# Turning an expert unit's outputs with one VectorE instruction and five transfers through DRAM

## The chip, the cores and the metric

The kernel runs on one core of a Trainium2 chip. The metric is device time in microseconds (us), lower is better. The engines named below are TensorE (PE; its weight loads are listed apart as PEld), VectorE (DVE), ScalarE (ACT), GpSimd (POOL) and SyncE (SP), which issues most of the transfers.

## The reference

Block-sparse attention (4 batches, 8 heads, 768 positions, head size 64, float32) is followed by a mixture of 8 experts without dropped tokens. The second part matters here:

```
x        = attention output as (3072, 512)
logits   = x @ w_gate                       # (3072, 8)
expert   = argmax(logits);  gate = softmax(logits)[expert]
for e in 8 experts:                         # rows grouped by expert
    y[rows of e] = relu(x[rows of e] @ w1[e]) @ w2[e]    # 512 -> 1024 -> 512
out = gate * y                              # in the rows' own order
```

Everything is float32. How many rows an expert gets is known only when the kernel runs.

## The kernel before

The attention part runs to about 358 us and writes its rows, with the gate as a 513th column, to a DRAM tensor `x_rows`. Then the rows are worked off in *units*, each a set of at most 512 rows of one expert: two `early` units of 256 rows, then `whole` units of 384 rows (here three, called unit0 to unit2), then one `own` unit per expert (own0 to own7) with what is left of that expert. The own units stand in a `tc.Switch` on their width, so that PE and ACT run code for the width that is needed; here it is 176, 128, 256, 128, 256, 160, 352 and 160 rows.

A unit goes through these steps, each a method of `Unit`:

- `gather` (L672): POOL fetches up to 4 x 128 rows from `x_rows` by index into the tile `xg`, rows on partitions.
- `fetch` (L686): SP fetches `w1` and `w2` of the expert, 2 MB each. Two pairs of buffers alternate.
- `turn` (L689, L697): DVE keeps the gates and turns the rows with 16 transposes of 32x32 blocks, into `xT` with features on partitions.
- `layer1` (L712, L716): 32 matmuls with `w1` as weights, relu on ACT into `hT`. The trace counts 64 for them, since it lists each float32 matmul twice.
- `layer2` (L725, L729): as many matmuls with 128 adjacent columns of `w2` as weights, output features on partitions, copied by ACT into `zT`.
- `finish` (L748, L753, L734): DVE turns `zT` back with 16 transposes into `zo`, POOL multiplies each group of 128 rows by the gates and puts it into the output by index. `zo` is one buffer.

The last unit, own7, uses `layer2_by_rows` (L765, L768, L734), whose outputs already have rows on partitions, so it has no `finish`.

PE, DVE and POOL are scheduled by hand: each executes its instructions in the order in which the code is written. SP is not; the scheduler orders it. The own loop's body is, for unit e: gather of e+2, the Switch with the two layers, `turn` of e+2, both fetches of e+2, `finish` of e. The buffers `xg`, `xT`, `zT` alternate from unit to unit. One `xg`, one `xT` and both `zT` are pieces of a large tile shown as `ar`; `hT` and `zo` are pieces of one shown as `ea`. So L697 has the two forms `xT<-ar` and `ar<-xg`.

Of the kernel before, what the change touches and what calls it, by code (L numbers as in the profile page):

```python
# [17 lines left out]
def kernel(  # L18
# [11 lines left out]
    nc = tc.nc  # L30
# [38 lines left out]

    x_d = nc.dram_tensor("x_rows", (N, XW), F32, kind="Internal").ap()  # L70


# [118 lines left out]
    by_hand = ExitStack()  # L191
    by_hand.enter_context(tc.manual_schedule(engines={mybir.EngineType.Pool, mybir.EngineType.PE, mybir.EngineType.DVE}))
    make_mask(make_mask_pool.enter_context(tc.tile_pool(name="mk", bufs=1)))
# [48 lines left out]
    def attend(n, half, c):  # L242
        v_sb = loaded[pairs[n]][2]
        if c == 0:

            ops_[(n, half)] = rt["bank"] = ps_o.tile([P, 512], F32, name="op")
        op = ops_[(n, half)][:, :CW]
        e = es[(n, half, c)]
        for hh in range(2):
            nc.tensor.matmul(  # L250
                op[hh * D : (hh + 1) * D, :], lhsT=v_sb[:, hh, c, :], rhs=e[:, hh, :], start=(c == 0), stop=(c == NCH - 1),
            )
        if c == NCH - 1:
            oT = work.tile([P, CW], F32, name="oT", bufs=4)
            nc.scalar.copy(oT[:], op)  # L255
            ops_[(n, half)] = oT

    def divide(n, half):

        oT, esum = ops_[(n, half)], esums.pop((n, half))  # L260
        sp = ps_x.tile([P, CW], F32, name="sp", tag="xr")
        for hh in range(2):
            nc.tensor.matmul(sp[hh * D : (hh + 1) * D, :], lhsT=ones[:], rhs=esum[:, hh, :], start=True, stop=True)
        ss = work.tile([P, CW], F32, name="ss")
        nc.scalar.activation(ss[:], sp[:], AF.Copy, bias=1e-9)  # L265
        row = 2 * (2 * n + half)
        nc.sync.dma_start(sums[row : row + 2, :], ss.rearrange("(h d) q -> h d q", h=2)[:, 0, :])
        r = work.tile([P, CW], F32, name="r")
        for m in range(HC):
            nc.vector.reciprocal(r[:, m * P : (m + 1) * P], ss[:, m * P : (m + 1) * P])  # L270
        nc.vector.tensor_mul(oT[:], oT[:], r[:])
# [381 lines left out]
    w2s = [wp.tile([P, FB, DM], F32, name=f"w2_{j}") for j in range(2)]  # L653
    xgs = [wp.tile([P, RJ, XW], F32, name="xg0")[:]]
    xTs = [wp.tile([P, DB, RW], F32, name="xT0")[:]]
# [3 lines left out]
    zo = flat[:, FB * RW : FB * RW + RJ * DM].rearrange("p (j d) -> p j d", j=RJ)  # L659
    zTs = [ar[:, j * DB * RW : (j + 1) * DB * RW].rearrange("p (c t) -> p c t", c=DB) for j in range(2)]  # L660
    xTs.append(ar[:, 2 * DB * RW : 3 * DB * RW].rearrange("p (c t) -> p c t", c=DB))
    xgs.append(ar[:, 3 * DB * RW : 3 * DB * RW + RJ * XW].rearrange("p (j w) -> p j w", j=RJ))

    class Unit:

        def __init__(self, ph, col, nj, at, expert, xg, xT, w, zT):
            self.ph, self.col, self.nj, self.at, self.expert = ph, col, nj, at, expert
            self.xg, self.xT, self.w1, self.w2, self.zT = xg, xTs[xT], w1s[w], w2s[w], zTs[zT]

        def gather(self):  # L670
# [49 lines left out]
        def layer2(self, n, between={}):  # L720

            for d in range(DB):
                zp = upper["banks"][(FB + d) % 6]
                for fb in range(FB):
                    nc.tensor.matmul(  # L725
                        zp[:, :n], lhsT=self.w2[:, fb, d * P : (d + 1) * P], rhs=hT[:, fb, :n],
                        start=(fb == 0), stop=(fb == FB - 1),
                    )
                nc.scalar.copy(self.zT[:, d, :n], zp[:, :n])  # L729
                for do in between.get(d, []):  # L730
                    do()
# [10 lines left out]

        def finish(self, group):

            for tq in range(4):
                for dq in range(4):
                    t, d = slice(tq * 32, (tq + 1) * 32), slice(dq * 32, (dq + 1) * 32)
                    nc.vector.transpose(  # L748
                        zo[t, : self.nj, :].rearrange("p j (c q d) -> p j c q d", c=DB, q=4)[:, :, :, dq, :],
                        self.zT[d].rearrange("p c (j q t) -> p j c q t", j=RJ, q=4)[:, : self.nj, :, tq, :],  # L750
                    )
            for j in range(self.nj):
                nc.gpsimd.tensor_scalar(  # L753
                    zo[:, j, :], zo[:, j, :], scalar1=gates[:, self.at, j : j + 1], scalar2=None, op0=ALU.mult,
                )
                self.put(j, zo[:, j, :], group)
# [32 lines left out]
    for i, (n, half) in enumerate(steps):  # L789
# [35 lines left out]
        if n + 1 == len(pairs) and half == 1:  # L825
# [3 lines left out]
            for j in range(QA // P):  # L829
                early[0].turn_by_matmul(j, tp[:, j])  # L830
    divide(*steps[-1])
    banks(lent)
# [11 lines left out]
    def tokens_b():  # L844
        judge()
        tokens("B", NT, NB_)
        whole(0, 0).fetch(1)
        whole(0, 0).gather()
        own[0].gather()

    rows_out(n, 0)
    early[0].layer1(QA, {2: [lambda: rows_out(n, 1)], 5: [turn_1], 7: [count_b]})
    early[0].layer2(QA)
    early[1].layer1(QA, {1: [tokens_b]})
    whole(0, 0).fetch(2)
    own[0].fetch(1)
    early[1].layer2(QA)
    own[0].fetch(2)
    whole(0, 0).turn()
    own[0].turn()  # L860
    for u in early:
        u.finish("rows_out")
    by_hand.close()

    lent.close()
    for arm in tc.Switch(nc.values_load(rt["arm"][0:1, 0:1], min_val=0, max_val=REDO), REDO + 1):
        inside = ExitStack()
        if arm <= UM:
            inside.enter_context(tc.manual_schedule(engines={mybir.EngineType.Pool, mybir.EngineType.PE, mybir.EngineType.DVE}))
            pools = inside.enter_context(ExitStack())  # L870
            banks(pools)
            units = [whole(i, arm - 1) for i in range(arm)]
            for u, then in zip(units, units[1:] + [own[1]]):
# [5 lines left out]
                then.fetch(2)  # L879
                u.finish("rows_out")  # L880
            if not units:
                own[1].gather()
                own[1].turn()
                own[1].fetch(1)
                own[1].fetch(2)
        else:
# [7 lines left out]
            for part in range(2):  # L894
                one_hots("A", rt["slA"], TA, EA * QA // P, part)
            tokens("A", TA, EA * QA // P)
            ranks("B", TA, NT)
# [3 lines left out]
            for u, width in [(u, QA) for u in early] + [(whole(i, i), UW) for i in range(UM)] + [(u, RW) for u in own]:  # L901
# [5 lines left out]
                u.layer2(width)  # L907
                u.finish("rows_again")

# [3 lines left out]
    banks(lent)  # L913
    by_hand.enter_context(tc.manual_schedule(engines={mybir.EngineType.Pool, mybir.EngineType.PE, mybir.EngineType.DVE}))
    ET = mybir.EngineType
    for e, u in enumerate(own):
        if e + 2 < E:
            own[e + 2].gather()
        at = rt["size"][0:1, e : e + 1]
# [6 lines left out]
        for k in tc.Switch(index, (RW - P) // GR + 1):  # L926
# [4 lines left out]
            else:  # L931
                u.layer2_by_rows(width, "rows_out")
        if e + 2 < E:
            own[e + 2].turn()
            own[e + 2].fetch(1)
            own[e + 2].fetch(2)
        if e + 1 < E:
            u.finish("rows_out")
    by_hand.close()
# [31 lines left out]
```

## Time and profile before

| | us |
|---|---|
| median of 3 runs | 899.52 |
| range of the runs | 899.34 to 901.68 |
| profiled execution, device time | 897.08 |
| profiled execution, span | 895.4 |
| PE busy in the span | 742.2 (83%) |
| DVE busy | 535.9 (60%) |
| POOL busy | 164.2 (18%) |

The span runs from the first to the last recorded instruction or transfer; all trace times are counted from its start. [...] A row's idle time names what ended it; "issue" there means that the engine waited for nothing that the profile shows.

### The profile page before, as it was taken

The numbers are of one execution on the slowest core, as the hardware profiler recorded it, in microseconds if no ns is written. First come the engines' busy times: TensorE is split into PE (matmuls) and PEld (weight loads), VectorE is DVE, ScalarE is ACT, GpSimd is POOL, SyncE is SP. The second block draws the span as 40 slices with busy tenths as digits, with TensorE's granted clock in tenths as the row PEclk, the third lists the DMA queues.
The fourth block names the chain that finished last, engine by engine and source line by source line (L and its number), as shares of the span: only waits on it lengthen the run. The fifth ranks groups of instructions, "written<-read, shape, count | busy, mean of one in ns | idle before, by whom it ended". The sixth has DMA issues, their size and how long they took to land. (4 is left out here: it accounts for less than half of the span.)

```text
span 895.4 us, 11949 instructions
## 1 busy us (share of the span) xinstructions
PE 742.2 (83%) x4516; PEld 481.7 (54%) x4516; DVE 535.9 (60%) x858; ACT 288.8 (32%) x516; POOL 164.2 (18%) x175
## 2 busy tenths in 40 slices
PE   7999999999999999999977999865970757189820
PEld 4555555555555555878544555864870657056600
DVE  4777787777777998478626443536272736363650
ACT  3666666666666665211101110110110101011100
POOL 4000000000000002011233131312314242323333
PEclk8999999999999999999998999976986797579875
DMA  7233232223222382155351434555454072402000
GB/s 160 71 80 80 74 73 72 72 72 73 72 72 72 112 320 78 26 207 167 134 183 67 142 117 155 195 182 197 147 180 157 12 250 84 159 14 59 18 13 35
DMA packets 98451, 99.74 MB, mean 111 GB/s; under 512 B 57491, under 2 KB 73939, under 8 KB 98324
## 3 DMA queue, kind: packets, MB, share of 16 engines
q1 hardware_dynamic: 89152, 79.50, 28.3%
q0 software_dynamic: 7040, 18.29, 6.5%
q8 instruction: 61, 1.00, 0.5%
q10 hardware_dynamic: 2132, 0.41, 0.2%
q14 instruction: 66, 0.54, 0.2%
HBM read 85.40 MB, written 17.66 MB: 115 GB/s over the span
## 5 line engine op out<-in xcount | busy, mean ns | idle before, releaser
L725 PE MATMUL bank<-ea,w 128*128 128x256 f32 (+5 forms) x768 | 170.8, 383 | 0.0
L229 PE MATMUL s<-ar 64*128 64x384 f32 x768 | 158.7, 492 | 0.9 <-ACT ar L214 0.9
L712 PE MATMUL bank<-xT,w 128*128 128x384 f32 (+3 forms) x512 | 121.6, 405 | 40.4 <-DVE xT L697 31.5
L234 ACT ACTIVATE ea<-s 128x768 f32<-128x768 f32 x192 | 152.4, 812 | 6.3 <-PE s L232 3.4
L725 PEld LDWEIGHTS bank<-ea,w 128*128 128x128 f32 x768 | 130.3, 191 | 38.8
L748 DVE STREAM_TRANSPOSE ea<-ar 32x512 f32<-32x512 f32 (+2 forms) x192 | 120.0, 625 | 35.9 <-DMA out_dram<-ea,sB 13.0
L712 PE MATMUL bank<-ar,w 128*128 128x256 f32 (+2 forms) x320 | 82.2, 423 | 64.9 <-DVE ar L697 51.4
L240 DVE TENSOR_TENSOR esum<-esum,ea 128x768 f32<-128x768 f32 x128 | 122.7, 958 | 14.1 <-ACT ea L234 0.5
L250 PE MATMUL op<-ea,ar 128*64 128x384 f32 x768 | 129.3, 486 | 0.0
L712 PEld LDWEIGHTS bank<-xT,w 128*128 128x128 f32 x512 | 91.2, 217 | 70.3 <-DVE xT L697 30.0
L716 ACT ACTIVATE ea<-bank 128x256 f32<-128x256 f32 (+5 forms) x104 | 38.8, 381 | 272.5 <-PE bank L712 249.9
L753 POOL TENSOR_SCALAR ea<-ea,gates 128x512 f32<-128x512 f32 x41 | 64.5, 1573 | 301.6 <-DVE ea L748 248.4
L712 PEld LDWEIGHTS bank<-ar,w 128*128 128x128 f32 x320 | 65.3, 214 | 80.7 <-DVE ar L697 51.8
L250 PEld LDWEIGHTS op<-ea,ar 128*64 128x64 f32 x768 | 55.1, 137 | 68.8 <-issue 68.8
L229 PEld LDWEIGHTS s<-ar 64*128 64x128 f32 x768 | 67.0, 190 | 38.1 <-issue 34.2
L270 DVE RECIPROCAL r<-ss 128x128 f32<-128x128 f32 x96 | 82.2, 911 | 2.5 <-ACT ss L265 2.5
L689 DVE COPY gates<-ar 128x4 f32<-128x4 f32 (+1 forms) x7 | 1.2, 170 | 125.3 <-DMA ar<-x_rows,gB 125.3
L697 DVE STREAM_TRANSPOSE xT<-ar 32x512 f32<-32x512 f32 (+1 forms) x112 | 72.3, 645 | 2.2
L240 DVE TENSOR_TENSOR esum<-ea 128x768 f32<-128x768 f32 x32 | 30.6, 957 | 63.4 <-ACT ea L234 63.4
L729 ACT COPY ar<-bank 128x256 f32<-128x256 f32 (+5 forms) x48 | 18.0, 375 | 149.9 <-PE bank L725 147.7
L232 PE MATMUL s<-pen,oh 64*128 64x384 bf16 x384 | 63.1, 325 | 0.0
L255 ACT COPY oT<-op 128x384 f32<-128x384 f32 x32 | 15.3, 478 | 106.3 <-PE op L250 106.3
(200 smaller groups left out, 455.4 us busy)
## 6 DMA issues: line engine op xcount, KB each, us to landing
w<-in_moe_w_dram SPq DMA_DIRECT2D x26, 2048.0 KB
ar<-in_k_dram SPq DMA_DIRECT2D x32, 192.0 KB
ar<-in_v_dram SPq DMA_DIRECT2D x16, 384.0 KB
x_rows<-xb SPq DMA_DIRECT2D x16, 384.0 KB
ar<-in_q_dram SPq DMA_DIRECT2D x30, 192.0 KB
out_dram<-ea,sB POOLq DMA_INDIRECT x37
sums<-ss SPq DMA_DIRECT2D x32, 3.0 KB
ar<-x_rows,gB POOLq DMA_INDIRECT x25
```

The costliest lines, as they stand in the source:

```text
L229: nc.tensor.matmul(s[:, hh, :CW], lhsT=kT[r, c * P : (c + 1) * P], rhs=qT[r, cols], start=True, stop=False)
L232: nc.tensor.matmul(s[:, hh, :CW], lhsT=oh[r, c, :], rhs=pen[r, cols], start=False, stop=True)
L234: nc.scalar.activation(e, s[:, :, :CW], AF.Exp, scale=scale)
L240: nc.vector.tensor_add(t[:], es[(n, half, 0)] if c == 1 else t[:], e)
L250: nc.tensor.matmul(op[hh * D : (hh + 1) * D, :], lhsT=v_sb[:, hh, c, :], rhs=e[:, hh, :], start=(c == 0), stop=(c == NCH - 1),)
L270: nc.vector.reciprocal(r[:, m * P : (m + 1) * P], ss[:, m * P : (m + 1) * P])
L697: nc.vector.transpose(self.xT[d].rearrange("p c (j q t) -> p j c q t", j=RJ, q=4)[:, : self.nj, :, tq, :], self.xg[t, : self.nj, :DM].rear ...
L712: nc.tensor.matmul(hp[:, :n], lhsT=self.w1[:, c, fb * P : (fb + 1) * P], rhs=self.xT[:, c, :n], start=(c == 0), stop=(c == DB - 1),)
L716: nc.scalar.activation(hT[:, fb, :n], hp[:, :n], AF.Relu)
L725: nc.tensor.matmul(zp[:, :n], lhsT=self.w2[:, fb, d * P : (d + 1) * P], rhs=hT[:, fb, :n], start=(fb == 0), stop=(fb == FB - 1),)
L748: nc.vector.transpose(zo[t, : self.nj, :].rearrange("p j (c q d) -> p j c q d", c=DB, q=4)[:, :, :, dq, :], self.zT[d].rearrange("p c (j q ...
L753: nc.gpsimd.tensor_scalar(zo[:, j, :], zo[:, j, :], scalar1=gates[:, self.at, j : j + 1], scalar2=None, op0=ALU.mult,)
```

## The change

`finish` is split. `turn_back` turns all of `zT` with a single DVE instruction into `zq`, in which each 32x32 block is transposed but stays in its group of 32 partitions. Its four column groups then go by four transfers, one from each group of 32 partitions, to their places in a DRAM tensor `z_rows`, and a fifth transfer loads `z_rows` into `zo`, rows on partitions. `leave` multiplies by the gates, now on DVE, and puts the rows. For the columns to come out in order, `layer2` takes every fourth column of `w2` as one set of 128 weights, so a weight load reads its floats 16 bytes apart, and `turn_back` writes with the same step.

There are two separate `xg` buffers. In the own loop the gather is issued for unit e+3 and stands ahead of the puts of unit e; the order on DVE becomes `turn_back` of e, `turn` of e+2, `leave` of e. SP is ordered by hand as well: the fetches of e+2 stand before the five transfers of e. Ahead of the units, `oT` has 3 buffers for 4, `r` 1 for 2, and the tokens of the second phase are worked out after block 3 and no longer after block 1 of the second early unit's first layer.

```diff
+    z_d = nc.dram_tensor("z_rows", (2, RW, DM), F32, kind="Internal").ap()
...
-            oT = work.tile([P, CW], F32, name="oT", bufs=4)
+            oT = work.tile([P, CW], F32, name="oT", bufs=3)
...
-        r = work.tile([P, CW], F32, name="r")
+        r = work.tile([P, CW], F32, name="r", bufs=1)
...
-    xgs = [wp.tile([P, RJ, XW], F32, name="xg0")[:]]
+    xgs = [wp.tile([P, RJ, XW], F32, name=f"xg{j}")[:] for j in range(2)]
...
+    zq = parts[3].rearrange("p (g d) -> p g d", g=4 * RJ)
...
-                        zp[:, :n], lhsT=self.w2[:, fb, d * P : (d + 1) * P], rhs=hT[:, fb, :n],
+                        zp[:, :n], lhsT=self.w2[:, fb, :].rearrange("p (d c) -> p c d", c=DB)[:, d, :], rhs=hT[:, fb, :n],
...
-        def finish(self, group):
-
-            for tq in range(4):
-                for dq in range(4):
-                    t, d = slice(tq * 32, (tq + 1) * 32), slice(dq * 32, (dq + 1) * 32)
-                    nc.vector.transpose(
-                        zo[t, : self.nj, :].rearrange("p j (c q d) -> p j c q d", c=DB, q=4)[:, :, :, dq, :],
-                        self.zT[d].rearrange("p c (j q t) -> p j c q t", j=RJ, q=4)[:, : self.nj, :, tq, :],
-                    )
+        def turn_back(self):
+
+            g = 4 * self.nj
+            nc.vector.transpose(
+                zq[:, :g, :].rearrange("p g (d c) -> p c g d", c=DB),
+                self.zT[:, :, : 32 * g].rearrange("p c (g t) -> p c g t", t=32),
+            )
+            for a in range(4):
+                nc.sync.dma_start(
+                    self.z_d[: 32 * g, a * P : (a + 1) * P].rearrange("(g t) d -> t g d", t=32), zq[a * 32 : (a + 1) * 32, :g, :],
+                )
+            nc.sync.dma_start(zo[:, : self.nj, :], self.z_d[: 32 * g].rearrange("(j p) d -> p j d", p=P))
+
+        def leave(self, group):
             for j in range(self.nj):
-                nc.gpsimd.tensor_scalar(
+                nc.vector.tensor_scalar(
                     zo[:, j, :], zo[:, j, :], scalar1=gates[:, self.at, j : j + 1], scalar2=None, op0=ALU.mult,
                 )
                 self.put(j, zo[:, j, :], group)
...
+    by_hand.enter_context(tc.manual_schedule(engines={mybir.EngineType.SP}))
     divide(*steps[-1])
...
-    early[1].layer1(QA, {1: [tokens_b]})
-    whole(0, 0).fetch(2)
+    first.fetch(2)
+    early[0].turn_back()
+    early[1].layer1(QA, {3: [tokens_b]})
     own[0].fetch(1)
     early[1].layer2(QA)
     own[0].fetch(2)
-    whole(0, 0).turn()
+    first.turn()
+    early[0].leave("rows_out")
+    early[1].turn_back()
     own[0].turn()
-    for u in early:
-        u.finish("rows_out")
+    early[1].leave("rows_out")
...
-                u.finish("rows_out")
+                u.turn_back()
+                if then is own[1]:
+                    own[2].gather()
+                u.leave("rows_out")
...
     for e, u in enumerate(own):
-        if e + 2 < E:
-            own[e + 2].gather()
...
+        if e + 3 < E:
+            own[e + 3].gather()
         if e + 2 < E:
-            own[e + 2].turn()
             own[e + 2].fetch(1)
             own[e + 2].fetch(2)
         if e + 1 < E:
-            u.finish("rows_out")
+            u.turn_back()
+        if e + 2 < E:
+            own[e + 2].turn()
+        if e + 1 < E:
+            u.leave("rows_out")
```

On DVE, two rounds of the own loop before the change; a branch marks the end of a round, L689 and L697 are `turn`, L748 is `finish`:

```order
L689 COPY gates<-ar 128x4
L697 STREAM_TRANSPOSE xT_178<-ar 32x4x4x32 x16
L748 STREAM_TRANSPOSE ea<-ar 32x16x32 x16
L966 UNCONDITIONAL_BRANCH
L689 COPY gates<-xg_177 128x4
L697 STREAM_TRANSPOSE ar<-xg_177 32x4x4x32 x16
L748 STREAM_TRANSPOSE ea<-ar 32x16x32 x16
L966 UNCONDITIONAL_BRANCH
```

and two rounds after it, where L751 is `turn_back`, L694 and L702 are `turn`, and L763 is the multiplication in `leave`, which the list shows in the stretch that follows its branch:

```order
L763 TENSOR_SCALAR ea<-ea,gates 128x512 x4
L751 STREAM_TRANSPOSE ar<-ar 128x4x512
L694 COPY gates<-xg_178 128x4
L702 STREAM_TRANSPOSE xT_179<-xg_178 32x4x4x32 x16
L988 UNCONDITIONAL_BRANCH
L763 TENSOR_SCALAR ea<-ea,gates 128x512 x4
L751 STREAM_TRANSPOSE ar<-ar 128x4x512
L694 COPY gates<-xg_177 128x4
L702 STREAM_TRANSPOSE ar<-xg_177 32x4x4x32 x16
L988 UNCONDITIONAL_BRANCH
```

The turning back of a unit stood behind the turn of the unit two ahead and stands before it now; its 16 instructions are one, and four multiplications have come from POOL.

On POOL, one round of the own loop before, with the multiplications (L753), puts (L734) and gather (L672):

```order
L753 TENSOR_SCALAR ea<-ea,gates 128x512
L734 DMA out_dram<-ea,sB 3072x512
L753 TENSOR_SCALAR ea<-ea,gates 128x512
L734 DMA out_dram<-ea,sB 3072x512
L753 TENSOR_SCALAR ea<-ea,gates 128x512
L734 DMA out_dram<-ea,sB 3072x512
L753 TENSOR_SCALAR ea<-ea,gates 128x512
L734 DMA out_dram<-ea,sB 3072x512
L672 DMA ar<-x_rows,gB 128x520 x4
L966 UNCONDITIONAL_BRANCH
```

and two rounds after, puts (L739) and gathers (L677):

```order
L739 DMA out_dram<-ea,sB 3072x512 x4
L677 DMA xg_177<-x_rows,gB 128x520 x4
L988 UNCONDITIONAL_BRANCH
L739 DMA out_dram<-ea,sB 3072x512 x4
L677 DMA xg_178<-x_rows,gB 128x520 x4
L988 UNCONDITIONAL_BRANCH
```

POOL's rounds hold no arithmetic any more, and what follows the puts of a unit is the gather for the unit four further on, where it was the one for three further on.

## Rows read from the trace of the kernel before

**Rows 1.** Timeline of PE, 455 to 870 us: start, length, line, operation, count, idle before.

```profile
474.72 22.83 PE L712 MATMUL bank<-xT,w 128*128 128x384 f32 x64 [9.49 <-DVE xT L697]
...
518.03 20.80 PE L712 MATMUL bank<-xT,w 128*128 128x384 f32 x64
...
573.95 9.84 PE L725 MATMUL bank<-ea,w 128*128 128x176 f32 x64
591.91 10.34 PE L712 MATMUL bank<-xT,w 128*128 128x128 f32 x64 [8.11 <-issue]
602.08 7.31 PE L725 MATMUL bank<-ea,w 128*128 128x128 f32 x64
619.86 16.79 PE L712 MATMUL bank<-ar,w 128*128 128x256 f32 x64 [10.47 <-DVE ea L748]
...
655.81 9.18 PE L712 MATMUL bank<-xT,w 128*128 128x128 f32 x64 [5.35 <-DVE xT L697]
...
699.32 16.34 PE L712 MATMUL bank<-ar,w 128*128 128x256 f32 x64 [27.18 <-DVE ar L697]
...
743.21 11.43 PE L712 MATMUL bank<-xT,w 128*128 128x160 f32 x64 [13.75 <-DVE xT L697]
754.48 8.86 PE L725 MATMUL bank<-ea,w 128*128 128x160 f32 x64
787.53 21.72 PE L712 MATMUL bank<-ar,w 128*128 128x352 f32 x64 [24.19 <-DVE ar L697]
...
831.11 11.84 PE L712 MATMUL bank<-xT,w 128*128 128x160 f32 x64 [2.92 <-DVE xT L697]
```

**Rows 2.** Who waited for whom, 560 to 860 us: us in total, times, longest.

```profile
POOL ea L753 <- DVE ea L748: 168.0, 6, 30.2
...
DVE gates L689 <- DMA xg<-x_rows,gB: 66.2, 3, 24.9
...
PE bank L712 <- DVE ar L697: 51.4, 2, 27.2
```

**Rows 3.** Timeline of DVE, 680 to 896 us, columns as in rows 1.

```profile
687.75 0.17 DVE L689 COPY gates<-xg 128x4 f32<-128x4 f32 x1 [20.25 <-DMA xg<-x_rows,gB]
687.83 11.44 DVE L697 STREAM_TRANSPOSE ar<-xg 32x512 f32<-32x512 f32 x16
699.29 11.71 DVE L748 STREAM_TRANSPOSE ea<-ar 32x512 f32<-32x512 f32 x16
...
855.77 11.71 DVE L748 STREAM_TRANSPOSE ea<-ar 32x512 f32<-32x512 f32 x16 [13.02 <-DMA out_dram<-ea,sB]
```

**Rows 4.** Timeline of POOL, 560 to 896 us.

```profile
683.42 0.95 POOL L672 DMA_INDIRECT xg<-x_rows,gB  x1 [0.31 <-issue]
...
867.58 1.56 POOL L753 TENSOR_SCALAR ea<-ea,gates 128x512 f32<-128x512 f32 x1 [13.06 <-DVE ea L748]
869.42 1.02 POOL L734 DMA_INDIRECT out_dram<-ea,sB  x1 [0.28 <-POOL ea L753]
...
883.51 0.98 POOL L734 DMA_INDIRECT out_dram<-ar,sB  x1 [0.30 <-issue]
```

**Rows 5.** Timeline of ACT, its last instruction.

```profile
856.84 0.68 ACT L768 ACTIVATE ar<-bank,gates 32x512 f32<-32x512 f32 x1 [6.30 <-PE bank L765]
```

**Rows 6.** DVE by line and shape, 240 to 400 us: busy us, mean ns, idle.

```profile
L511 DVE TENSOR_REDUCE slA<-slot 128x18 f32<-128x144 f32 x1 | 0.4, 399 | 0.0
...
L378 DVE TENSOR_SCALAR ok<-sums 64x384 f32<-64x384 f32 x1 | 0.3, 345 | 0.0
...
L441 DVE TENSOR_REDUCE best<-sc 128x18 f32<-128x144 f32 x1 | 0.3, 303 | 0.0
```

**Rows 7.** Weight loads by line and shape, 380 to 860 us.

```profile
L633 PEld LDWEIGHTS <-orB 128*128 128x128 bf16 x24 | 1.3, 103 | 1.3 <-issue 1.3
```

**Rows 8.** Busy time by stage: each engine, then clock, DMA share, GB/s.

```profile
560.00:592.00 32.00, 20.84 (x128) 20.33 (x126) 11.29 (x20) 3.22 (x12) 11.71 (x10) 0.88 0.66 232
...
743.00:788.00 45.00, 20.59 (x129) 20.35 (x130) 23.20 (x35) 3.59 (x12) 14.31 (x12) 0.69 0.34 121
```

More of the change, by code (lines that the diff above doesn't have):

```diff
@@ L191 @@
     by_hand = ExitStack()
-    by_hand.enter_context(tc.manual_schedule(engines={mybir.EngineType.Pool, mybir.EngineType.PE, mybir.EngineType.DVE}))
+    BY_HAND = {mybir.EngineType.Pool, mybir.EngineType.PE, mybir.EngineType.DVE}
+    by_hand.enter_context(tc.manual_schedule(engines=BY_HAND))
     make_mask(make_mask_pool.enter_context(tc.tile_pool(name="mk", bufs=1)))
@@ L659 @@
     zo = flat[:, FB * RW : FB * RW + RJ * DM].rearrange("p (j d) -> p j d", j=RJ)
-    zTs = [ar[:, j * DB * RW : (j + 1) * DB * RW].rearrange("p (c t) -> p c t", c=DB) for j in range(2)]
-    xTs.append(ar[:, 2 * DB * RW : 3 * DB * RW].rearrange("p (c t) -> p c t", c=DB))
-    xgs.append(ar[:, 3 * DB * RW : 3 * DB * RW + RJ * XW].rearrange("p (j w) -> p j w", j=RJ))
+    parts = [ar[:, j * DB * RW : (j + 1) * DB * RW] for j in range(4)]
+    xTs.append(parts[0].rearrange("p (c t) -> p c t", c=DB))
+    zTs = [parts[j].rearrange("p (c t) -> p c t", c=DB) for j in (1, 2)]
+    zq = parts[3].rearrange("p (g d) -> p g d", g=4 * RJ)
     class Unit:
@@ L668, in __init__ @@
             self.xg, self.xT, self.w1, self.w2, self.zT = xg, xTs[xT], w1s[w], w2s[w], zTs[zT]
+            self.z_d = z_d[zT]
         def gather(self):
@@ L846, in tokens_b @@
         tokens("B", NT, NB_)
-        whole(0, 0).fetch(1)
-        whole(0, 0).gather()
+        first.gather()
         own[0].gather()
+    first = whole(0, 0)
     rows_out(n, 0)
     early[0].layer1(QA, {2: [lambda: rows_out(n, 1)], 5: [turn_1], 7: [count_b]})
+    first.fetch(1)
     early[0].layer2(QA)
-    early[1].layer1(QA, {1: [tokens_b]})
-    whole(0, 0).fetch(2)
+    first.fetch(2)
+    early[0].turn_back()
+    early[1].layer1(QA, {3: [tokens_b]})
     own[0].fetch(1)
@@ L868 @@
         if arm <= UM:
-            inside.enter_context(tc.manual_schedule(engines={mybir.EngineType.Pool, mybir.EngineType.PE, mybir.EngineType.DVE}))
+            inside.enter_context(tc.manual_schedule(engines=BY_HAND | {mybir.EngineType.SP}))
             pools = inside.enter_context(ExitStack())
@@ L879 @@
                 then.fetch(2)
-                u.finish("rows_out")
+                u.turn_back()
+                if then is own[1]:
+                    own[2].gather()
+                u.leave("rows_out")
             if not units:
+                own[2].gather()
                 own[1].gather()
@@ L895 @@
                 one_hots("A", rt["slA"], TA, EA * QA // P, part)
-            tokens("A", TA, EA * QA // P)
+            tokens("A", TA, EA * QA // P, redo=True)
             ranks("B", TA, NT)
@@ L907 @@
                 u.layer2(width)
-                u.finish("rows_again")
+                u.turn_back()
+                u.leave("rows_again")
             nc.vector.memset(rt["sB"][:], 2 * N)
@@ L913 @@
     banks(lent)
-    by_hand.enter_context(tc.manual_schedule(engines={mybir.EngineType.Pool, mybir.EngineType.PE, mybir.EngineType.DVE}))
+    by_hand.enter_context(tc.manual_schedule(engines=BY_HAND | {mybir.EngineType.SP}))
     ET = mybir.EngineType
     for e, u in enumerate(own):
-        if e + 2 < E:
-            own[e + 2].gather()
         at = rt["size"][0:1, e : e + 1]
@@ L937 @@
         if e + 1 < E:
-            u.finish("rows_out")
+            u.turn_back()
+        if e + 2 < E:
+            own[e + 2].turn()
+        if e + 1 < E:
+            u.leave("rows_out")
     by_hand.close()
```

## The prediction, made before the changed kernel was run

> **What bounds the kernel now.** I read the timeline of PE first, because PE does the work that cannot be shortened, and looked for the places where it stands still. Up to about 358 us it is busy and the change leaves its work there alone, so only the units count. In their rows the reader is to see the number in square brackets: PE waited 9.49 us before unit1, nothing before unit2, and then before own1 to own7 8.11, 10.47, 5.35, 27.18, 13.75, 24.19 and 2.92 us, in sum 91.97 [rows 1]. The rows of the long ones name DVE's L697 as what ended them: the turn of the rows that the unit is about to multiply.
>
> The waits say what DVE waited for in turn. It waited for gathered rows (66.2 us in three waits for the one buffer), and POOL, which issues the gathers, waited 168.0 us for DVE's L748, the turning back [rows 2]. The timeline of DVE shows the ring: the gates come at 687.75 after a wait for the gather, the turn takes 11.44 us, and the turning back of the unit before, long since computed, follows for 11.71 us [rows 3]. Only then can POOL multiply (1.56 us a group) and put (1.02 us a group), and only behind that stands the next gather [rows 4]. One lap takes 11.44 + 11.71, four times 2.9 for multiplying and putting, four issues of a gather at about 1.3 and some 4 until the rows can be used: 44 us, longer than most units take on PE. So in the units a ring through DVE, POOL and a gather sets the pace.
>
> The end has the same ring: the last turning back starts at 855.77 after waiting 13.02 us for earlier puts [rows 3], though ACT, and with it all computing, ends at 857.52 [rows 5]. POOL then multiplies and puts own6, and only then own7; its last put starts at 883.51 [rows 4], 11.89 us before the span's end.
>
> **The change, part by part.**
>
> *The ring is cut.* The gather moves ahead of the puts and one unit earlier; in a row with 20.25 us of waiting [rows 3] that is more than enough, since the last issue of a gather at 683.42 lay 4.3 us before its rows were used [rows 4]. The turn of e+2 then runs right behind the turning back of e, some 16 us after unit e ends on PE, and unit e+1 still has to be computed before it is needed. Every unit then finds its rows turned. What is late next is PE's own entry into the Switch: before own1 it waited 8.11 us for nothing that the profile shows [rows 1], and the 10.47 us of own2 are put down to an L748 that no matmul of that unit reads, so I count both as the price of entry. For own3 and own7 the entry costs no more than the gaps seen, 5.35 and 2.92; half of them is taken. For own4, own5 and own6 it is hidden, from nothing to 10.47 each; I take the mean of the four visible gaps, 6.7. Sum left: 8.1 + 10.5 + 2.7 + 3 x 6.7 + 1.5 = 42.9. Saved: 91.97 - 42.9 = **49.1 us** (between 27 and 74 by the two ends).
>
> Before unit1 no Switch is entered; 9.49 us go, and its first layer, 22.83 us where unit2's took 20.80 [rows 1], gets 2.0 back: **11.5 us**. I do not book such a return in the own units. own7's first layer takes 11.84 us after a gap of only 2.92, against 8.86 for own5's second layer, which has the same width [rows 1]; short gaps cost it too.
>
> *The turning back itself.* 512 floats a partition take 732 ns (11.71 us / 16) [rows 3], 1.43 ns each, so 2,048 take 2.9 us. Written 16 bytes apart they cost more: the reduction L511, which reads 144 floats 72 bytes apart, takes 399 ns, and L441, on as many adjacent ones, 303 [rows 6], 0.67 ns more per float. With that it is 4.3 us. The multiplication comes to DVE: L378 takes 345 ns for 384 floats [rows 6], so four of 512 take 1.8 us. DVE has about 17.5 us of work a unit where it had 23.2, beside PE, so neither end matters.
>
> *The way through DRAM.* It adds 1 MB written and 1 MB read per unit. The trace has no store of this kind. With 232 GB/s at a DMA share of 0.66 [rows 8] the engines together would give some 350 GB/s: 3 us each way; if 32 partitions only get half, 6. Each hop also takes what a gather took from issue to use, 3 to 4 us. Behind the w2 fetch that is sent as unit e ends (2 MB, 6 us), the rows stand in `zo` some 20 to 25 us after unit e's end. What waits: SP, with the next fetches queued behind it, and DVE in `leave`, with the next turning back behind it. The fetches of e+3 are wanted only when unit e+1 has freed its buffers, and the next turning back when e+1 is done, 26 us or more later (own1's layers, 10.34 + 7.31, and an entry). Price **0**, and up to 30 us if the transfers are later than that (below).
>
> *The weights of layer 2.* Each load now reads 128 floats 16 bytes apart. No load in the trace does. From below it costs nothing. From the rows: a load of 128 adjacent columns takes 103 ns [rows 7], and 128 x 0.67 = 86 ns for the step of the DVE pair make 189. Loads overlap matmuls, so only units whose matmuls are shorter than a load pay. Per matmul own1 takes 114 ns (7.31 us / 64), own5 138, own0 154 [rows 1]; from unit2's 325 for 384 columns follow 217 for 256 and 298 for 352, which hide it. Paid: own1 and own3 64 x 75 = 4.8 us each, own5 3.3, own0 2.2: **15.1 us**.
> [...]
>
> *The end.* own6's rows are in `zo` by the time own7 has been computed (no weights are fetched any more), so own7's puts follow ACT's last instruction. From 857.52 to the start of the last put at 883.51 lie 26.0 us; 0.3 stay: **25.7 us**.
>
> *The rest.* The tokens of the second phase come two of a layer's eight blocks later, 16 x 217 ns = 3.5 us, and DVE's turn for unit0 ended more than that before PE came to it. `oT` and `r` are written in an order in which the buffer lost was not yet needed again: 0, and by the busy PE there some us at most if not.
>
> **Sum**, from the profiled execution's 897.08 (its span 895.4 and 1.7 around it): 897.1 - 11.5 - 49.1 - 25.7 + 15.1 = 825.9. The median of the runs shown is 2.4 above that execution, so I say 826 without adding it.
>
> **The rivals.**
>
> *The strided load is free.* For it: the pair of rows is DVE's, and no row ties PE's loads to it. Against: that pair is all that the trace has on such a step. Time: 825.9 - 15.1 = 810.8.
>
> *Transfers become the bound.* An own unit moves 4.2 MB of weights, 1 MB gathered, 1 MB put and 2.1 MB through DRAM, 8.3 MB, and at 232 GB/s, the higher of the two stages shown (the other has 121) [rows 8], that is 36 us, where PE would have some 29 on average (230 us for eight). For it: puts and gathers of 2 KB rows crowd with the fetches. Against: the DMA share was 0.66 there and not 1, and the last two units have no weights to fetch. If it holds in the four units own2 to own5, 4 x 7 = 28 us: 854.
>
> *Slower: the weight load becomes the bound of all layer 2.* With a load of t ns, the 12 units with this layer pay 64 x the excess over 217 (twice), 325 (three times), 154, 114, 217, 114, 217, 138 and 298 ns, which sum to 2,662. The gains of 86.3 us are eaten when 12t - 2,662 = 86,300 / 64 = 1,348, so t = 334 ns, over three times the 103. At four times, 412 ns, the price is 64 x (4,944 - 2,662) = 146 us: 957. For it: nothing but that the trace has no such load; against it, that DVE's step costs a third.
>
> *It does not do what it says:* some wait (SP behind the z transfers, one `zo`) closes a new ring of the same length, and only the end and unit1 gain: 897.1 - 37.2 + 15.1 = 875, still faster; without those gains too, no change.
>
> **How the numbers follow.** Forecast (826, its own range 812 to 840) 0.45, free load 0.27, transfers 0.16, new ring 0.06 (of which 0.02 without any gain), slower 0.06. The range leaves out the last two and the outer part of the ends: 803, below the free load with cheaper entries, to 858, above the transfers' case. A measurement tells apart about 0.3%, 2.7 us. Faster 0.92, same 0.02, slower 0.06.
>
> **What would show it.** PE's gaps before own4 and own6 at most about 10 us, with a releaser other than L702, and none before unit1. On PE, matmuls of own1's second layer at about 189 ns (12.1 us for 64) and unit2's unchanged at 20.8. On DVE one transpose of 3 to 5 us per unit. POOL's gathers done well before the turn that reads them, and the last put within 2 us of ACT's end. If second layers of 384 columns lengthen, the load is over 325 ns and the slower case holds; if PE waits for weights, the transfers' case; if own1's second layer stays at 7.3 us, the load is free.

## The result, and the profile after

The changed kernel takes 817.72 us (median of 4 runs, 815.24 to 819.0) against 899.43 for the kernel before on the same chip: ratio 0.9084, 95% interval 0.9057 to 0.9111. The profiled execution took 817.38, its span is 815.7. The forecast was 826, range 803 to 858.

The timeline of PE in the changed kernel answers to [rows 1]. Columns are start, length, engine, line, operation, shapes, count and, in brackets, the idle time before and what ended it. L717 is a first layer, L730 a second one.

```profile
406.41 15.09 PE L730 MATMUL bank<-ea,w 128*128 128x256 f32 x64
...
463.73 20.80 PE L717 MATMUL bank<-xT,w 128*128 128x384 f32 x64
...
548.75 11.46 PE L717 MATMUL bank<-ar,w 128*128 128x176 f32 x64 [2.30 <-DVE xT L702]
560.05 15.10 PE L730 MATMUL bank<-ea,w 128*128 128x176 f32 x64
579.52 9.40 PE L717 MATMUL bank<-xT,w 128*128 128x128 f32 x64 [4.37 <-DVE ar L751]
588.75 15.09 PE L730 MATMUL bank<-ea,w 128*128 128x128 f32 x64
611.17 15.67 PE L717 MATMUL bank<-ar,w 128*128 128x256 f32 x64 [7.33 <-issue]
...
644.06 9.01 PE L717 MATMUL bank<-xT,w 128*128 128x128 f32 x64 [2.28 <-issue]
...
674.79 16.29 PE L717 MATMUL bank<-ar,w 128*128 128x256 f32 x64 [6.79 <-issue]
...
708.94 10.61 PE L717 MATMUL bank<-xT,w 128*128 128x160 f32 x64 [2.94 <-issue]
719.39 15.09 PE L730 MATMUL bank<-ea,w 128*128 128x160 f32 x64
737.49 20.79 PE L717 MATMUL bank<-ar,w 128*128 128x352 f32 x64 [3.01 <-issue]
...
778.16 8.93 PE L717 MATMUL bank<-xT,w 128*128 128x160 f32 x64 [0.95 <-issue]
786.93 14.01 PE L775 MATMUL bank<-w,ea 128*128 128x512 f32 x32
```

Three things are to be seen. unit1 follows unit0 without a wait, where it waited 9.49 us. The waits before own1 to own7 are 4.37, 7.33, 2.28, 6.79, 2.94, 3.01 and 0.95 us, in sum 27.7 where there were 92.0; most are now put down to "issue", nothing that the profile shows. And every second layer of up to 256 rows takes 15.1 us, whether it has 128, 160, 176 or 256 rows: a matmul every 236 ns.

On DVE the ring of [rows 3] is gone. One unit's turning back (L751), a turn (L702) and the multiplication (L763):

```profile
706.45 3.82 DVE L751 STREAM_TRANSPOSE ar<-ar 128x2048 f32<-128x2048 f32 x1 [14.85 <-ACT ar L734]
...
710.12 11.43 DVE L702 STREAM_TRANSPOSE ar<-xg 32x512 f32<-32x512 f32 x16
724.23 1.68 DVE L763 TENSOR_SCALAR ea<-ea,gates 128x512 f32<-128x512 f32 x4 [2.68 <-DMA ea<-z_rows]
```

The turn begins as soon as the turning back is done, with no wait for its rows; what is waited for is the load from `z_rows`, 2.68 us here. The rows of this unit, own4, are in `zo` 17.8 us after its last copy (706.45 to 724.23); for own0 to own5 it is 17.7 to 21.6 us. From 545 to 800 us DVE waits 50.6 us for such loads, eight times and at most 12.7 us. The end, on ACT and then on POOL, answers to [rows 4, 5]:

```profile
800.98 0.68 ACT L778 ACTIVATE ar<-bank,gates 32x512 f32<-32x512 f32 x1 [6.29 <-PE bank L775]
```

```profile
798.97 0.98 POOL L739 DMA_INDIRECT out_dram<-ea,sB  x1 [0.30 <-issue]
802.26 0.98 POOL L739 DMA_INDIRECT out_dram<-ar,sB  x1 [2.31 <-ACT ar L778]
803.55 0.98 POOL L739 DMA_INDIRECT out_dram<-ar,sB  x1 [0.30 <-issue]
```

own6's last put stands ahead of ACT's end now, and own7's last put starts 1.9 us after it, where it was 26.0 us. The transfers are busier than before [rows 8]. A stretch of 25 us, with busy time of PE, PEld, DVE, ACT and POOL, granted clock (1.00 is full speed), DMA share and GB/s:

```profile
575.00:600.00 25.00, 20.63 (x114) 20.51 (x113) 16.55 (x22) 2.85 (x11) 5.08 (x5) 0.86 0.83 281
```

The share is 0.83, at 281 GB/s, and yet no unit waits for weights by name.

### The profile page after: what moved, and what is told of

The parts are those of the page before. It is cut to its first block, busy times and chain, and to the rows that moved or that the text cites. A ratio compares the mean times of both kernels' runs of the same rounds, so it can differ in the third digit from the quotient of the medians.

```text
span 815.7 us, 11938 instructions
## 1 busy us (share of the span) xinstructions
PE 762.7 (94%) x4516; PEld 541.2 (66%) x4516; DVE 471.1 (58%) x719; ACT 288.0 (35%) x516; POOL 98.6 (12%) x134
## 4 chain that ended last, share of the span: by engine, by line
PE 80%; DMA 10%; issue 4%; DVE 4%; POOL 1%; ACT 1%; SPq 0%; POOLq 0%; DVEq 0%; ACTq 0%
PE bank L730 19%; PE bank L717 17%; PE s L231 16%; PE op L252 15%; DMA out_dram<-ea,sB 6%; PE s L234 4%; PE sp L265 3%; PE xr L285 3%; PE tp L214 2%; DVE ar L751 2%; DMA z_rows<-ar 2%; DVE xT L702 1%; DMA ea<-z_rows 1%; DMA xg<-x_rows,gB 1%; SPq L756 0%
## 5 line engine op out<-in xcount | busy, mean ns | idle before, releaser
L730 PE MATMUL bank<-ea,w 128*128 128x256 f32 (+5 forms) x768 | 202.5, 425 | 0.0
L730 PEld LDWEIGHTS bank<-ea,w 128*128 128x128 f32 x768 | 198.2, 322 | 3.3
L717 PE MATMUL bank<-xT,w 128*128 128x384 f32 (+3 forms) x512 | 114.7, 388 | 11.4 <-issue 7.0
L717 PEld LDWEIGHTS bank<-xT,w 128*128 128x128 f32 x512 | 85.5, 204 | 39.3 <-issue 8.3
L717 PE MATMUL bank<-ar,w 128*128 128x256 f32 (+2 forms) x320 | 78.4, 410 | 19.4 <-issue 17.1
L751 DVE STREAM_TRANSPOSE ar<-ar 128x2048 f32<-128x2048 f32 (+2 forms) x12 | 39.5, 3295 | 94.3 <-ACT ar L734 88.1
L717 PEld LDWEIGHTS bank<-ar,w 128*128 128x128 f32 x320 | 63.2, 207 | 33.6 <-issue 21.6
L734 ACT COPY ar<-bank 128x256 f32<-128x256 f32 (+5 forms) x48 | 18.1, 376 | 181.7 <-PE bank L730 170.3
L702 DVE STREAM_TRANSPOSE xT<-xg 32x512 f32<-32x512 f32 (+1 forms) x112 | 72.2, 645 | 2.2
L739 POOL DMA_INDIRECT out_dram<-ea,sB x37 | 37.2, 1007 | 271.4 <-DVE ea L763 263.2
L242 DVE TENSOR_TENSOR esum<-ea 128x768 f32<-128x768 f32 x32 | 30.6, 958 | 62.6 <-ACT ea L236 62.6
L763 DVE TENSOR_SCALAR ea<-ea,gates 128x512 f32<-128x512 f32 x41 | 17.3, 483 | 75.9 <-DMA ea<-z_rows 75.9
```

What stands on the lines that cost most here:

```text
L242: nc.vector.tensor_add(t[:], es[(n, half, 0)] if c == 1 else t[:], e)
L702: nc.vector.transpose(self.xT[d].rearrange("p c (j q t) -> p j c q t", j=RJ, q=4)[:, : self.nj, :, tq, :], self.xg[t, : self.nj, :DM].rear ...
L717: nc.tensor.matmul(hp[:, :n], lhsT=self.w1[:, c, fb * P : (fb + 1) * P], rhs=self.xT[:, c, :n], start=(c == 0), stop=(c == DB - 1),)
L730: nc.tensor.matmul(zp[:, :n], lhsT=self.w2[:, fb, :].rearrange("p (d c) -> p c d", c=DB)[:, d, :], rhs=hT[:, fb, :n], start=(fb == 0), sto ...
L739: ins = nc.gpsimd.indirect_dma_start(out=out[:, :], out_offset=bass.IndirectOffsetOnAxis(ap=rt["s" + self.ph][:, self.col + j : self.col + ...
L751: nc.vector.transpose(zq[:, :g, :].rearrange("p g (d c) -> p c g d", c=DB), self.zT[:, :, : 32 * g].rearrange("p c (g t) -> p c g t", t=32),)
```

## The experiments

Ten kernels were run. Each time is a median of 4 to 6 runs (one run for the step of 8 bytes) with the kernel before beside it, whose runs took 895 to 901 us throughout; in brackets are the ratio to that kernel and its 95% interval. The changed kernel has 817.7. Where a diff is cut, dots say so.

**The order of the gathers alone.** In the kernel before, only the gathers move.

```diff
+                if then is own[1]:
+                    own[2].gather()
                 u.finish("rows_out")
...
-        if e + 2 < E:
-            own[e + 2].gather()
...
+        if e + 3 < E:
+            own[e + 3].gather()
         if e + 2 < E:
             own[e + 2].turn()
```

> The kernel before with one thing changed: the gather of own unit e+3 is issued ahead of unit e's puts (own2's ahead of the last whole unit's). The 16-instruction turning back, the multiplication on POOL and adjacent weights stay. Theory: the order of the gathers alone cuts the ring of DVE, POOL and gather in the own units; the waits before own1 to own7 fall from 92 to about 43, own6's rows are put while own7 is computed (-23), unit1 still waits 9.5: 899.4 - 49 - 23 = about 827 us. Rival: DVE's 23.2 us and POOL's 12 per unit still set the pace without the single instruction, waits named L697 or L748 stay before own4 and own6, and the time is 870 or more.

827.06 us (ratio 0.9196, 0.9169 to 0.9223), as the theory had it. Its PE:

```profile
474.98 23.06 PE L712 MATMUL bank<-xT,w 128*128 128x384 f32 x64 [9.66 <-DVE xT L697]
...
591.50 9.24 PE L712 MATMUL bank<-xT,w 128*128 128x128 f32 x64 [8.59 <-DVE ar L697]
...
618.20 16.27 PE L712 MATMUL bank<-ar,w 128*128 128x256 f32 x64 [10.31 <-issue]
...
681.98 16.80 PE L712 MATMUL bank<-ar,w 128*128 128x256 f32 x64 [12.00 <-DVE ea L748]
...
746.16 20.57 PE L712 MATMUL bank<-ar,w 128*128 128x352 f32 x64 [9.86 <-DVE ea L748]
```

unit1 still waits 9.66 us, and the waits before own1 to own7 fall to 45.6 in sum, none over 12.0. So an order of instructions, with DVE's and POOL's work as it was, brings 72 us where the whole change brought 82.

**The late gather in the changed kernel.** The opposite: all of the change but that order.

```diff
-                if then is own[1]:
-                    own[2].gather()
                 u.leave("rows_out")
...
+        if e + 2 < E:
+            own[e + 2].gather()
         at = rt["size"][0:1, e : e + 1]
...
-        if e + 3 < E:
-            own[e + 3].gather()
```

> The changed kernel, but own unit e+2 is gathered at the top of the round of unit e, as before, and so behind the puts of unit e-1 only. Theory: the way through DRAM is done some 20 us after a unit's end and the puts 6 us later, so the gather lands about 10 us into the next unit but one's lead, and the turn still ends before PE needs it: no change, 816 to 822 us; the ring can be cut by either edit. Rival: without the early gather the ring closes again, POOL in front of the gather waiting for the way through DRAM: PE waits for L702 before own2 to own6, 840 or more.

817.45 us (0.9108, 0.9082 to 0.9134): no difference.

```profile
608.88 15.53 PE L717 MATMUL bank<-ar,w 128*128 128x256 f32 x64 [5.06 <-DVE ar L751]
...
671.41 16.68 PE L717 MATMUL bank<-ar,w 128*128 128x256 f32 x64 [4.77 <-DVE ar L751]
```

These two waits, before own2 and own4, are its longest, 5.06 and 4.77 us, under those of the changed kernel. The ring is cut by the order of the gathers alone, and by the rest of the change without it; the two gains do not add. Which part of that rest suffices (the single instruction, its place ahead of the turn, the multiplication on DVE, the second `xg` buffer, SP's order by hand) was not run apart.

**Adjacent weights.** The step of 16 bytes is taken out of the changed kernel's loads, and the columns are put in order by DVE's multiplication.

```diff
-    lhsT=self.w2[:, fb, :].rearrange("p (d c) -> p c d", c=DB)[:, d, :]
+    lhsT=self.w2[:, fb, d * P : (d + 1) * P]
...
-    zq[:, :g, :].rearrange("p g (d c) -> p c g d", c=DB)
+    zq[:, :g, :].rearrange("p g (c d) -> p c g d", c=DB)
...
-    zo[:, j, :], zo[:, j, :], scalar1=...
+    self.rows[:, j, :].rearrange("p (c a d) -> p a c d", c=DB, a=4),
+    zo[:, j, :].rearrange("p (a c d) -> p a c d", c=DB, a=4), scalar1=...
...
-    self.put(j, zo[:, j, :], group)
+    self.put(j, self.rows[:, j, :], group)
```

> The changed kernel, but layer 2 takes 128 adjacent columns of w2 per weight load again, and DVE's multiplication by the gates puts the columns in order (runs of 32 floats, into the unit's zT). In the changed kernel each of the 64 listed matmuls of a second layer of up to 256 rows took 236 ns, 15.1 us per layer, where before 7.3 to 14.0 were needed: own1 and own3 +7.8 each, own5 +6.2, own0 +5.3, four layers of 256 rows +1.1 each, 31.5 us in all. Theory: that is the weight load with the step of 16 bytes, and while PE works it off, part of the entry into the next Switch is hidden; the seven waits before own1 to own7, 27.7 us in the changed kernel, grow back to about 43. Then 817.7 - 31.5 + 15 = about 801 us. Rival 1: the entry costs the same whatever PE does before it; the waits stay at 27.7 and the time is about 786. Rival 2: the second layers are slow for another reason (transfers that run beside them); they stay at 15.1 and the time at about 818.

810.36 us (0.902, 0.8994 to 0.9047): a version that beats the changed kernel too. But only 7.4 us of the 31.5 came; the theory, at 801, had 16.5.

```profile
577.93 7.57 PE L718 MATMUL bank<-xT,w 128*128 128x128 f32 x48 [8.90 <-DMA w<-in_moe_w_dram]
...
588.75 7.31 PE L731 MATMUL bank<-ea,w 128*128 128x128 f32 x64
606.96 16.93 PE L718 MATMUL bank<-ar,w 128*128 128x256 f32 x64 [10.90 <-DMA w<-in_moe_w_dram]
...
669.20 16.54 PE L718 MATMUL bank<-ar,w 128*128 128x256 f32 x64 [10.93 <-DMA w<-in_moe_w_dram]
```

The second layer is back at 7.31 us for 128 rows, so rival 2 (transfers) falls. The waits before own1 to own7 grow to 49.8: 8.90, 10.90 and 10.93 before own1, own2 and own4 where they were 4.37, 7.33 and 6.79, and 11.40 before own6 where it was 3.01. Three of them name a transfer of weights, and the experiment cannot tell such a wait from the entry, which lasts as long in the kernel before (8.11 and 10.47 before the same units, [rows 1]). ACT waited 13.6 us for puts, which here read from `zT` (`self.rows` is a view of it); that cost is this version's own.

**The step alone, in the kernel before.** Its output columns come in another order.

```diff
-    lhsT=self.w2[:, fb, d * P : (d + 1) * P]
+    lhsT=self.w2[:, fb, :].rearrange("p (d c) -> p c d", c=DB)[:, d, :]
```

> The kernel before with one thing changed: a weight load of layer 2 takes every fourth column of w2, with a step of 16 bytes; so its output columns stand in another order. Theory: every second layer of up to 256 rows takes 15.1 us as in the changed kernel, 31.5 us more PE work in all, but before own4, own5 and own6 PE waited for the ring and before own1 and own2 for the entry, which hide most of it: 2 to 12 us more than 899.4. Rival 1: the load is only slow beside the transfers of the changed kernel; second layers stay at 7.3 to 14.0 us and the time at 899. Rival 2: the ring turns with PE and the whole 31 us are paid: 931.

906.89 us (1.0086, 1.0058 to 1.0113): 7.4 us slower, inside the theory's 2 to 12.

```profile
590.40 5.60 PE L712 MATMUL bank<-xT,w 128*128 128x128 f32 x48 [1.41 <-issue]
598.35 2.05 PE L712 MATMUL bank<-xT,w 128*128 128x128 f32 x16 [2.35 <-ACT ea L716]
600.24 15.09 PE L725 MATMUL bank<-ea,w 128*128 128x128 f32 x64
617.64 15.61 PE L712 MATMUL bank<-ar,w 128*128 128x256 f32 x64 [2.31 <-DVE ea L748]
...
704.70 16.45 PE L712 MATMUL bank<-ar,w 128*128 128x256 f32 x64 [23.05 <-DVE ar L697]
```

The layer of 128 rows takes 15.09 us here too, without any transfer through `z_rows`: the price comes from the step of the load. The waits before own1 and own2 shrink from 8.11 and 10.47 to 1.41 (with 2.35 more inside that layer, for ACT) and 2.31, and the one for the ring before own4 from 27.18 to 23.05.

**A step of 8 bytes** (columns in another order, one run).

```diff
-    lhsT=self.w2[:, fb, :].rearrange("p (d c) -> p c d", c=DB)[:, d, :]
+    lhsT=self.w2[:, fb, (d // 2) * 256 : (d // 2 + 1) * 256].rearrange("p (k c) -> p c k", c=2)[:, d % 2, :]
```

> The changed kernel with a step of 8 bytes in layer 2's weight loads in place of 16 (every second column of a half of w2; the output's columns stand in another order). [...] Rival 1: any step but one float costs the same 236 ns a load: 15.1 us. Rival 2: the cost goes with the bytes passed over, half of the surplus: about 11 us.

816.5 us. The layer answers more sharply than the total:

```profile
588.14 7.70 PE L730 MATMUL bank<-ea,w 128*128 128x128 f32 x64
607.68 15.60 PE L717 MATMUL bank<-ar,w 128*128 128x256 f32 x64 [11.84 <-DMA w<-in_moe_w_dram]
```

7.70 us, 120 ns a matmul, where adjacent floats gave 7.31 and the step of 16 gave 15.09. Rival 1 and rival 2 (11 us) fall. Half the step costs half the time (118 of 236 ns, near the 120 measured); a price by all the bytes that a load passes over would give that, but no run shows the cause. The records of the loads agree. These are own1's second layers with a step of 16 bytes, of 8, and with adjacent floats (busy us, then mean ns of one):

```profile
L730 PEld LDWEIGHTS bank<-ea,w 128*128 128x128 f32 x64 | 15.0, 330 | 0.0
L730 PEld LDWEIGHTS bank<-ea,w 128*128 128x128 f32 x64 | 7.6, 196 | 0.0
L731 PEld LDWEIGHTS bank<-ea,w 128*128 128x128 f32 x64 | 7.2, 192 | 0.0
```

A record is longer than the pace (192 ns at a load every 114), so successive loads overlap, and a record's length is not what a load costs. Again nearly nothing reached the total: own2 waited 11.84 us.

**No Switch.** The widths of these inputs as constants.

```diff
...
-        for k in tc.Switch(index, (RW - P) // GR + 1):
-            width = P + k * GR
...
+        width = (176, 128, 256, 128, 256, 160, 352, 160)[e]
```

> The changed kernel without the Switch of the own units: the widths of these inputs (176, 128, 256, 128, 256, 160, 352, 160) are constants. Theory: the waits before own1 to own7 in the changed kernel (4.4, 7.3, 2.3, 6.8, 2.9, 3.0, 1.0, in sum 27.7) are the price of entering the Switch; they vanish, and with them a few us of first layers at the lower clock: 817.7 - 28 - 3 = about 787 us. Rival: rows or weights come late as well; waits named L702 or a transfer of weights stay, and less than half of the 27.7 goes: 804 or more.

770.38 us (0.8571, 0.8549 to 0.8593), 47.3 less, where 31 were expected.

```profile
570.67 7.31 PE L717 MATMUL bank<-xT,w 128*128 128x128 f32 x64
577.81 15.09 PE L730 MATMUL bank<-ea,w 128*128 128x128 f32 x64
592.74 13.98 PE L717 MATMUL bank<-ar,w 128*128 128x256 f32 x64
```

PE has no wait from 546.19 to its end. The 27.7 us of waits and own0's 2.30 are gone, 13 us of first layers came back as well (own1's takes 7.31 us for 9.40), and the end is 3.0 us shorter. The first layers were slower for the clock: where own1's ran in the changed kernel, the granted clock was 0.77 on average (the column after POOL's), and 0.77 of its 9.40 us is 7.2; over the whole span it rises from 0.971 to 0.996 without the Switch.

```profile
579.60:588.60 9.00, 9.00 (x63) 9.00 (x64) 8.82 (x14) 1.74 (x7) 0.00 (x0) 0.77 1.01 326
```

Own1 and own2 start 22.1 us apart here and still find rows and weights in time, so those of the changed kernel, at 31.7 us, are in time too; what is left of its gaps is the price of the Switch. What that price consists of is not shown. One thing differs in the list of DMA queues: the queue q8, of kind "instruction", moved 1.00 MB in 61 packets with the Switch and 0.64 MB in 39 without.

**No Switch and adjacent weights.**

> The changed kernel with both edits of the two runs before: adjacent columns in layer 2's loads (DVE's multiplication puts the columns in order) and constant widths, no Switch, in the own units. Alone the first gave 7.4 us and the second 47.3. Theory: slow loads and the entry into the Switch cover each other; with no entry there is nothing left to cover the loads, and all of their 31.5 us come back: 770.4 - 31.5 = about 739 us, PE without gaps. Rival: at that pace the transfers (8.3 MB per own unit, 23 us of PE) become the bound; waits for weights or rows appear, and the time is 755 or more.

753.15 us (0.8374, 0.8345 to 0.8403), 14 over the theory's 739 and just under the rival's 755. One stretch of 40 us, columns as in the stretch above:

```profile
660.00:700.00 40.00, 35.34 (x171) 27.70 (x171) 25.62 (x38) 6.07 (x17) 12.33 (x12) 0.91 0.94 319
```

Waits of PE before own1 and own6, and of DVE before the multiplication that stands ahead of own6's turn:

```profile
570.42 7.09 PE L718 MATMUL bank<-xT,w 128*128 128x128 f32 x48 [5.82 <-ACT ar L735]
...
680.13 22.18 PE L718 MATMUL bank<-ar,w 128*128 128x352 f32 x64 [4.66 <-DVE ar L703]
```

```profile
664.78 1.67 DVE L764 TENSOR_SCALAR ar<-ea,gates 128x512 f32<-128x512 f32 x4 [10.24 <-DMA ea<-z_rows]
```

And what ACT waited for (us in total, times, longest):

```profile
ACT ar L735 <- DMA out_dram<-ar,sB: 24.6, 5, 16.4
```

The loads now count: 17.2 us against 7.4 under the Switch. Much of the rest stays in waits on transfers, whose share is 0.94 at 319 GB/s: DVE waits 10.24 us for a load from `z_rows` and so turns own6's rows late (4.66 us, and a first layer of 22.18 us for 19.10). ACT waits 24.6 us for puts out of `zT`, a wait that this version of the loads has made itself, and PE's 5.82 us before own1 are put down to ACT's copies into `zT`. How much more a version without that detour would gain was not run.

**The order alone, and no Switch.**

> The kernel before with the gathers ahead of the puts (827.1 us) and with constant widths, no Switch, in the own units: turning back by 16 instructions, multiplication on POOL, adjacent loads. With PE without gaps it would take about 739 plus what this kernel keeps from before, unit1's wait with its slow first layer 11.5 and the early tokens 3.5: 754 us. Theory: with no entry to wait for, DVE's 23.2 us per unit (own units take PE 23 on average, the short ones 14.6) is the bound: PE waits for L697, and the time is 765 to 780; the single instruction and the way through DRAM are worth that much more than they showed under the Switch. Rival: DVE keeps up, 754.

791.1 us (0.8807, 0.8792 to 0.8822), over the 765 to 780 of the theory, which had left the end out: from PE's last matmul to the span's end it takes 22.8 us, against 11.7 in the changed kernel without the Switch.

```profile
701.03 22.18 PE L712 MATMUL bank<-ar,w 128*128 128x352 f32 x64 [6.12 <-DVE ar L697]
```

PE waits for L697 as the theory said, 6.18, 4.10 and 6.12 us before own2, own4 and own6. So with the entry gone, what the change has beyond the order (the single instruction, the way through DRAM, the second gather buffer, the later tokens) is worth 20.7 us even with its slow loads (791.1 against 770.4); under the Switch it was worth 9.3 (827.1 against 817.7).

**The tokens after block 1 again.**

```diff
-    early[1].layer1(QA, {3: [tokens_b]})
+    early[1].layer1(QA, {1: [tokens_b]})
```

> The changed kernel with the tokens of the second phase worked out after block 1 of early[1]'s first layer again, as before, and not after block 3. From the start of that layer to the start of its second layer PE took 19.05 us before (with waits for L382 and L385 of DVE) and 15.59 after; the prediction had priced the move at nothing. Theory: PE waits there for DVE, which now also has a turning back in front of that work; the stretch grows by 3 to 5 us and all later work with it: 821 to 823 us. Rival: what follows has slack, or the waits came from something else; 817 to 818.

821.64 us (0.914, 0.9111 to 0.9169), as the theory had it.

```profile
391.77 3.62 PE L717 MATMUL bank<-ar,w 128*128 128x256 f32 x16
396.77 0.17 PE L385 MATMUL okp<-notok,all__1252 64*128 64x1 bf16 x1 [1.38 <-DVE notok L384]
...
411.25 15.09 PE L730 MATMUL bank<-ea,w 128*128 128x256 f32 x64
```

From the first layer's start (391.77) to the second's (411.25) 19.5 us pass, and 15.6 in the changed kernel (390.82 to 406.41). The single runs spread more than elsewhere, 818.3 to 826.3 us; the stretch itself is the firmer evidence.

**The multiplication on POOL again.**

```diff
-                nc.vector.tensor_scalar(
+                nc.gpsimd.tensor_scalar(
                     zo[:, j, :], zo[:, j, :], scalar1=gates[...]
```

> The changed kernel with the multiplication by the gates on POOL again, 1.58 us a group for 0.42 on DVE. Theory: puts end some 5 us later after each unit, which nothing waits for before the end; own6's puts then run into own7's, and the end comes 3 to 5 us later: 820 to 823 us. Rival: POOL's longer round delays gathers and the loads into the one zo, and PE waits again: 830 or more.

832.08 us (0.926, 0.9221 to 0.9298), 14.4 more: the rival's number, and partly its mechanism.

```profile
466.04 20.91 PE L717 MATMUL bank<-xT,w 128*128 128x384 f32 x64 [2.07 <-DVE xT L702]
```

```profile
814.31 1.03 POOL L739 DMA_INDIRECT out_dram<-ea,sB  x1 [0.28 <-POOL ea L763]
```

Of the 16.2 us between the two spans 6.8 are the end: own6's last put (814.31) stands behind own7's computing (PE ends at 810.4, the span at 831.9). The other 9.4 are spread over waits such as unit1's 2.07 for L702, whose gather stands behind the early puts on POOL, and own2's 8.68 (7.33 in the changed kernel), and over slower first layers; which of them POOL caused was not taken further.

## Why the prediction was right, point by point

The direction and the range held, and so did the mechanism of the ring, of unit1 and of the end. That 826 came within 8 us is in part luck: two errors of 15 and 16 us nearly cancelled, and smaller terms did the rest. The terms are from the two profiled executions. The end goes by the last line of PE in the changed kernel and by this one of the kernel before:

```profile
842.78 14.01 PE L765 MATMUL bank<-w,ea 128*128 128x512 f32 x32
```

| term | forecast, us | measured, us |
|---|---|---|
| waits before own1 to own7 | -49.1 | 92.0 to 27.7: -64.3 |
| unit1, wait and first layer | -11.5 | -11.5 |
| weight loads of layer 2 | +15.1 | +31.5 |
| end, from PE's last matmul on | -25.7 | 38.6 to 14.7: -23.9 |
| own0's wait, first layers of the own units | 0 | -7.9 |
| tokens two blocks later | 0 | -3.5 |
| sum | -71.2 | -79.6 of the spans' -79.7 |

*The ring* was read rightly from the three timelines. Its lap, added up to 44 us, is seen in [rows 1]: own4 to own7 start 43.5, 43.9, 44.3 and 43.6 us after the unit before them, whatever their width. The prediction put the ring's end down to the gather's new place; that is one of two sufficient causes, since the late gather gave the same time.

*The entry into the Switch* was the step that was mis-sized: 42.9 us stayed in the forecast, 27.7 in the run. Kernels without the ring but with adjacent or nearly adjacent loads have 45.6 (order alone), 49.8 (adjacent) and 53.9 (step of 8), close to the forecast. In them the wait is mostly long behind a short second layer and short behind a long one: in the kernel with the order alone 8.6 to 12.0 us before own1, own2, own4 and own6, which follow second layers of 7.3 to 9.7 us, and 0.7 to 3.2 before own3, own5 and own7, which follow 14.0 to 19.1. Slow loads lengthen the short layers, and so hide part of the entry: before own2, PE waited 10.3 to 11.8 us when own1's second layer took 7.3 to 7.7, and 2.3 to 8.7 when it took 15.1, in nine kernels. The length of the whole unit before fits as well as that of its second layer: in the changed kernel the waits before own2 and own3, 7.33 and 2.28 us, both follow second layers of 15.1 us, while own1 and own2 as a whole took 24.3 and 30.6. In the seven kernels with the Switch and without the ring, own1 to own6 start 26.7 to 37.7 us after the unit before them, 31.4 on average. The mechanism behind this relation is not shown.

*The weight load* was the other: 189 ns forecast, 236 measured. DVE's pair had the direction, though it is no clean pair (L511 is a sum, L441 a maximum). The base of the sum was misread: the 103 ns of [rows 7] are a load of bf16, and the loads of `w2` are float32, whose records last 191 ns on average in the kernel before and 322 in the changed kernel, and overlap, so neither number is what a load adds to the pace. The result was a fifth too low; the short layers paid 3 us more each than priced, the four of 256 rows 1.1 us each, and the term doubled. The three loads that were measured: a step of 16 bytes 236 ns, of 8 bytes 120, adjacent at most 114.

*Turning back*: 3.8 us by L751 for a forecast of 2.9 to 4.3; 1.7 us for four multiplications against 1.8. The rows stood in `zo` 18 to 22 us after a unit's end, in the 20 to 25 forecast or better. DVE waited for the z transfers, 50.6 us in all, but no wait of PE is put down to them, so the price of 0 held; the transfers' rival came near only when the Switch and the slow loads were both taken out. The 230 us of PE for eight own units in that rival are in no row; in the changed kernel 252 us pass from own0's start to PE's end.

*The tokens* were priced at nothing because the turn that follows has slack. The cost was elsewhere: PE itself had waited for DVE there, and the run with the old place takes 3.9 us more. *Moving the multiplication* was priced as free room on DVE; what it takes off POOL, worth 14 us, was not looked at.

## What to carry to other kernels

Where engines wait for each other in a ring, look for the cheapest instruction order that cuts it first: here a gather issued one round earlier, ahead of the puts, brought 72 us by itself where the whole change brought 82. Price two costs that can overlap, such as a slow layer and the entry into the code that follows, together: each looked like some 30 us, and removing the slow loads alone gave 7. When PE reads weights with a step, price the load from rows of the same type and shape, and compare it with the matmul that has to cover it: here matmuls of 352 and 384 rows covered a step of 16 bytes (19.1 and 20.8 us a layer, as without it), and those of 256 and fewer did not (15.1 us for 14.0 and less).

## What the runs showed of the hardware

With float32 weights of 128 columns, matmuls of 128 rows follow each other every 236 ns when the floats lie 16 bytes apart, every 120 ns at 8 bytes and every 114 ns when they are adjacent; the first number is the same with and without the transfers through `z_rows`. The step of 16 bytes, in its writes, costs DVE two thirds more in the single transpose: 3.82 us for 2,048 floats above, and with adjacent writes, in the adjacent version:

```profile
699.99 2.31 DVE L752 STREAM_TRANSPOSE ar<-ar 128x2048 f32<-128x2048 f32 x1 [15.97 <-ACT ar L735]
```

The Switch over eight units cost 47 us in the changed kernel, more than the 30 us of waits that the timeline shows in front of them: 13 us more went to the first layers behind those waits, at a lower granted clock (0.77 in own1's), and 3 to the end. Its price depends on the rest: with adjacent weights it was 57 us (810.36 to 753.15), in the kernel before with the new order 36 (827.06 to 791.1).
